# Chunk attention and a phase MLP on one core: fp32 weight loads on SyncE's queue, merged q/k copies, and a new written order

## The chip, the cores and the metric

The kernel runs on one core of one Trainium2 chip. The metric is the device time of one execution in microseconds (us). A core has five engines that run at the same time, each through its own list of instructions in order: TensorE (PE in the profile; PEld is its weight load), VectorE (DVE), ScalarE (ACT), GpSimd (POOL) and SyncE (SP). Transfers are issued from the POOL and SP queues here. An engine waits for another's result only where an instruction says so.

## The reference

Inputs are q, k and v of shape (8 batches, 8 heads, 576 rows, 64), and four weights. Attention runs inside chunks of 64 rows, with no link between chunks. Its result, seen as (8, 576, 512), goes through a phase MLP that mixes all 576 rows of a batch:

```python
scores = scale * np.matmul(q_c, k_c.transpose(0, 1, 2, 4, 3))   # per chunk of 64 rows
attn = np.exp(scores - max); attn = attn / (np.sum(attn) + 1e-09)
x = np.matmul(attn, v_c)                                        # -> (8, 576, 512)
theta = x @ w_theta
zr, zi = x * np.cos(theta), x * np.sin(theta)
y = einsum('ts,bsd->btd', w_tok_r, zr) + einsum('ts,bsd->btd', w_tok_i, zi)
u = x + y
out = u + np.maximum(u @ w_ch, 0.0)
```

w_theta and w_ch are 512 x 512, w_tok_r and w_tok_i 576 x 576. All inputs and the output are fp32 in HBM; the kernel computes in fp16 with fp32 sums.

## The kernel before, in words

**Tiling.** Batches are taken in four pairs, 0 to 3. A pair has 2 x 576 rows, which is nine tiles of 128 rows by 512 columns. Tiles 0 to 3 belong to the first batch, 5 to 8 to the second, and tile 4 holds the last 64 rows of both. Loads and attention work on five groups of a pair: A (tiles 0, 1), B (2, 3), M (4), C (5, 6) and D (7, 8).

**The order is written out by hand.** The string `ORDER` (L18) is a list of steps, and the loop at its end (L568) emits them one by one, with `work` (L525) as the table from a step's name to its function. A step such as `T.0M.1` is kind T, pair 0, group M, PSUM slot 1; `Y.05.1` is pair 0, tile 5. Each engine and each queue runs its own instructions in the order in which this list emits them, so a step that waits holds everything behind it on its engine. Nothing is reordered later.

**The steps of a group.** `q`, `k`, `v` (L170, L179) load from HBM on POOL's queue, and the transfer casts fp32 to fp16; each step is two DMAs. `T` (L250) transposes q and k of a group on PE into one PSUM tile. `tq` and `tk` (L268) copy the q half and the k half of that tile to SBUF, q on DVE, k on ACT (both on DVE for group M). `S` (L281) makes the scores, `e` (L297) their exp on ACT, `V0` and `V1` (L310) multiply with v for four heads each, and `v0` and `v1` (L329) divide by the sum on DVE, which gives x. `X` (L346) transposes x on PE, and `x` (L361) copies it out on ACT; or `Xd` (L370) does both as one DMA transpose on SP's queue. `H` (L381) is x times w_theta, `g` (L397) its cosine and sine on ACT, `z` (L412) the two products on DVE, and `zm` (L428) moves two half tiles for group M by DMA.

**The steps of a tile.** `Y` (L438) sums nine products of the transposed token weights with zr and zi; at the start of the kernel it is cut into `Ya`, `Yb`, `Yc`. `y` (L462) adds x on DVE and gives u. `U` (L469) transposes u on PE and `u` (L484) copies it out, on DVE for odd tiles and ACT for even ones; or `Ud` (L479) does it by DMA on SP's queue. `W` (L493) is u times w_ch, `w` (L503) is the relu and the last sum on DVE, and `st` (L511) stores with two DMAs on SP's queue.

**The weights.** `lw.00` (L187) loads all of w_tok_r in fp32 on SP's queue, and `cw` (L197) casts it on ACT; `lw.01` loads w_tok_i on POOL's queue with a cast. `TW` (L206) transposes the token weights on PE, three 128-row blocks of the result at a time, into one PSUM tile; `twd` and `twa` (L232) copy it out on DVE and ACT. `lt` and `lc` (L201) load w_theta and w_ch on POOL's queue with a cast. `D` (L154) is two blank matmuls of 512 columns, whose result nobody reads. `init` (L139) makes the identity for the transposes, on POOL.

**Buffers.** PSUM has three tiles of two banks (slots 0 to 2 of T, S, V, X, H, TW) and two of one bank (slots 0 and 1 of Y, U, W, D). SBUF tiles come from rings: seven for loaded q and k, six for u, four for the transposed u. A new use of a ring's buffer waits until its last reader is done.

The softmax here doesn't subtract the row's maximum and nothing guards it: scores larger than these inputs give would overflow.

## Time and profile before

| | |
|---|---|
| median of 4 runs | 212.46 us (211.46 to 213.87) |
| the profiled execution | 211.46 us, its span 209.7 us |
| PE busy | 190.5 us, 91% of the span |
| DVE busy | 123.5 us, 59% |
| ACT busy | 111.3 us, 53% |
| POOL busy | 104.3 us, 50% |
| moved by DMA | 31.36 MB, of which 15.88 MB on POOL's queue (with a cast) |
| q, k and v loads | 120 DMAs on POOL's queue, some 0.87 us each to issue |

The span runs from the first to the last instruction of the core. "Busy" is the time in which an engine had an instruction under way. The chain that ended last is followed back from the last instruction, at each step to what released it.

### The profile page before, as it was taken

How to read it: one execution, taken by the hardware profiler on the slowest of the kernel's cores; microseconds unless marked ns; L12 is line 12 of the kernel's file. 1: busy time of each engine (PE TensorE's matmuls, PEld its weight loads, DVE VectorE, ACT ScalarE, POOL GpSimd, SP SyncE). 2: the span in 40 equal slices, each digit the busy share in tenths (PEclk: the TensorE clock that was granted, in tenths of full speed). 3: DMA queues.
4: the chain of work that ended last, by engine and by line, in shares of the span. 5: the costliest groups of instructions: out<-in, count | busy, mean ns of one | idle time of the engine just before them, and what ended most of it. 6: DMA issues, size and time to landing. Idle time of an engine off the chain costs nothing.

```text
span 209.7 us, 6370 instructions
## 1 busy us (share of the span) xinstructions
PE 190.5 (91%) x2774; PEld 96.2 (46%) x2774; DVE 123.5 (59%) x240; ACT 111.3 (53%) x119; POOL 104.3 (50%) x130
## 2 busy tenths in 40 slices
PE   7797698897989999999999999998999979999981
PEld 2335354454545555455544545444544424444430
DVE  0015646464958756677885356949876465846351
ACT  2516587845796588777558668785250531500010
POOL 8998889997997789798998300000000000000000
PEclk9958799999999999999999999999999999999998
DMA  6999999999999999999999992425228687636875
GB/s 190 189 149 172 186 155 163 161 155 156 151 158 202 213 144 172 165 178 157 178 191 194 173 184 52 105 50 103 54 64 174 125 173 147 152 64 129 175 155 129
DMA packets 136858, 31.36 MB, mean 150 GB/s; under 512 B 129536, under 2 KB 131648, under 8 KB 136832
## 3 DMA queue, kind: packets, MB, share of 16 engines
q0 software_dynamic: 114176, 15.88, 120.1%
q1 hardware_dynamic: 22656, 15.10, 31.5%
q8 instruction: 21, 0.34, 0.7%
q14 instruction: 5, 0.04, 0.1%
HBM read 33.06 MB, written 9.44 MB: 203 GB/s over the span
## 4 chain that ended last, share of the span: by engine, by line
PE 65%; DVE 9%; ACT 9%; DMA 7%; POOL 6%; issue 1%; SPq 0%; POOLq 0%; ACTq 0%
PE ps_y L457 27%; PE ps_theta L388 14%; PE ps_uw L497 13%; POOL qk L174 5%; DMA v<-in_v_dram 4%; PE ps_x L323 3%; DMA xT<-x 3%; ACT kT L277 3%; PE ps_qkT L259 3%; PE ps_sT L290 2%; DVE qT L277 2%; DVE x L336 2%; PE ps_xT L354 2%; ACT xT L366 1%; PE ps_uT L474 1%
## 5 line engine op out<-in xcount | busy, mean ns | idle before, releaser
L457 PEld LDWEIGHTS <-wT 128*128 128x128 f16 (+1 forms) x360 | 30.7, 100 | 34.5 <-issue 0.8
L457 PE MATMUL ps_y<-zr,wT 128*128 128x512 f16 (+1 forms) x180 | 44.3, 381 | 0.0
L457 PE MATMUL ps_y<-zi,wT 128*128 128x512 f16 (+1 forms) x180 | 42.0, 379 | 0.0
L465 DVE TENSOR_TENSOR u<-ps_y,x 128x512 f16<-128x512 f32 x36 | 24.7, 689 | 27.9 <-PE ps_y L457 27.8
L497 PE MATMUL ps_uw<-wch,uT 128*128 128x512 f16 x144 | 36.3, 380 | 1.2 <-ACT uT L491 0.7
L388 PE MATMUL ps_theta<-wtheta,xT 128*128 128x512 f16 x144 | 35.1, 386 | 1.7 <-DMA xT<-x 1.3
L174 POOL DMA_DIRECT2D qk<-in_q_dram x40 | 34.2, 872 | 4.9 <-DMA qk<-in_q_dram 1.3
L174 POOL DMA_DIRECT2D qk<-in_k_dram x40 | 33.9, 868 | 4.8 <-DMA v<-in_v_dram 1.4
L182 POOL DMA_DIRECT2D v<-in_v_dram x40 | 34.1, 872 | 3.0 <-DMA qk<-in_k_dram 1.3
L506 DVE SCALAR_TENSOR_TENSOR o<-ps_uw,u 128x512 f32<-128x512 f32 x36 | 24.8, 688 | 16.1 <-PE ps_uw L497 15.8
L404 ACT ACTIVATE cos<-ps_theta,pihalf 128x1024 f16<-128x1024 f32 (+1 forms) x20 | 20.6, 1032 | 21.7 <-PE ps_theta L388 15.2
L303 ACT ACTIVATE eT<-ps_sT 128x1024 f16<-128x1024 f32 (+1 forms) x20 | 18.4, 938 | 16.5 <-PE ps_sT L290 16.4
L336 DVE TENSOR_TENSOR x<-ps_x,recip 128x512 f16<-128x512 f32 (+1 forms) x40 | 25.5, 638 | 1.4
L388 PEld LDWEIGHTS <-xT 128*128 128x128 f16 x144 | 13.4, 99 | 17.6 <-DMA xT<-x 2.3
L497 PEld LDWEIGHTS <-uT 128*128 128x128 f16 x144 | 13.0, 98 | 16.7 <-DMA uT<-u 1.4
L277 ACT COPY kT<-ps_qkT 128x1024 f16<-128x1024 f16 x16 | 16.1, 1018 | 7.8 <-DVE qT L277 4.4
L366 ACT COPY xT<-ps_xT 128x1024 f16<-128x1024 f16 (+1 forms) x15 | 13.9, 931 | 10.8 <-PE ps_xT L354 10.7
L408 ACT ACTIVATE sin<-ps_theta 128x1024 f16<-128x1024 f32 (+1 forms) x20 | 18.7, 937 | 0.0
L491 ACT COPY uT<-ps_uT 128x512 f16<-128x512 f16 x9 | 5.3, 592 | 24.3 <-PE ps_uT L474 24.2
L277 DVE COPY qT<-ps_qkT 128x1024 f16<-128x1024 f16 x16 | 11.0, 688 | 9.2 <-ACT kT L277 6.6
L259 PE MATMUL ps_qkT<-id,qk 64*128 64x64 f16 x576 | 12.8, 196 | 1.2 <-ACT sin L408 0.8
L335 DVE RECIPROCAL recip<-ps_x 128x8 f32<-128x8 f32 (+1 forms) x40 | 7.8, 196 | 9.9 <-PE ps_x L323 9.6
(43 smaller groups left out, 152.8 us busy)
## 6 DMA issues: line engine op xcount, KB each, us to landing
out_dram<-o SPq DMA_DIRECT2D x72, 128.0 KB, 2.5
qk<-in_q_dram POOLq DMA_DIRECT2D x32, 128.0 KB, 7.0
qk<-in_k_dram POOLq DMA_DIRECT2D x32, 128.0 KB, 7.0
v<-in_v_dram POOLq DMA_DIRECT2D x32, 128.0 KB, 6.7
wraw<-in_moe_w_tok_r_dram SPq DMA_DIRECT2D x1, 1152.0 KB
wnat<-in_moe_w_tok_i_dram POOLq DMA_DIRECT2D x1, 576.0 KB, 7.9
qk<-in_q_dram POOLq DMA_DIRECT2D x8, 64.0 KB, 6.4
qk<-in_k_dram POOLq DMA_DIRECT2D x8, 64.0 KB, 6.2
```

The source lines that it names most:

```text
L174: nc.gpsimd.dma_start(nats[p, g][rows, which, r], (q, k)[which][b, :, t0 : t0 + n, :].rearrange("h s d -> s h d"),)
L182: nc.gpsimd.dma_start(v16[rows, slot + r, :, 0:D], v[b, :, t0 : t0 + n, :].rearrange("h s d -> s h d"),)
L259: nc.tensor.transpose(psv[:, r, w, e, j, :], t[half[r], w, j, 2 * e : 2 * e + 2, :].rearrange("s h d -> s (h d)"), id16[half[r], half[r]],)
L277: copy(out=t.rearrange(flat), in_=ps.rearrange(flat))
L336: nc.vector.tensor_tensor(out=st[p]["x"][:, j0 : j0 + n, f * NE * D : (f + 1) * NE * D].rearrange("p c (h d) -> p c h d", h=NE), in0=psv[: ...
L388: nc.tensor.matmul(ps[:, j * DM : j * DM + DM], xT[:, j * NDB + db, :], wtheta16[:, db, :], start=(db == 0), stop=(db == NDB - 1),)
L404: nc.scalar.activation(out=cos[:, 0:n].rearrange("p a e -> p (a e)"), in_=pin, func=AF.Sin, bias=pihalf, scale=1.0,)
L408: nc.scalar.activation(out=sin[:, 0:n].rearrange("p a e -> p (a e)"), in_=pin, func=AF.Sin)
L457: nc.tensor.matmul(ps[rows], wT[:, kt, cols], z[:, jz, :], start=(kt == 0), stop=(kt == 2 * KT),)
L465: nc.vector.tensor_tensor(out=u, in0=st[p].pop(("ps_y", j))[:, 0:DM], in1=st[p]["x"][:, j], op=ALU.add)
L497: nc.tensor.matmul(ps, uT[:, db * P : db * P + P], wch16[:, db, :], start=(db == 0), stop=(db == NDB - 1),)
L506: nc.vector.scalar_tensor_tensor(out=o, in0=st[p].pop(("ps_uw", j)), scalar=0.0, in1=u, op0=ALU.max, op1=ALU.add)
```

## The change

The change has six parts.

1. **Token weights.** `load_tok` now has four steps. `lw.00` and `lw.01` load rows 0 to 255 of w_tok_r and w_tok_i in fp32 on SP's queue; `lw.02` and `lw.03` load the other rows (256 to 511, and 512 to 575) on POOL's queue with a cast. `cw.00` and `cw.01` cast the fp32 halves on DVE. The fp32 tile borrows the buffer that pair 1's zr uses later. `TW` has four steps, two for each part of the rows, and all its copies (`twd`) are on DVE; `twa` is gone.
2. **Phase weight.** `lt` loads w_theta in fp32 on SP's queue, into the buffer that pair 1's x uses later, and `ct` casts it on ACT.
3. **q and k copies.** The two copies of a transposed group become one over the whole PSUM tile: `tq` on DVE (15 groups), `tqa` on ACT (5 groups). `Td`, a DMA transpose of q and k, is defined but the order doesn't use it.
4. **Other copies.** The copy of transposed x is on DVE in nine groups (`xv`) and on ACT in five (`x`); group 2B is transposed by DMA (`Xd.2B`). The copy of transposed u is on ACT (`ua`) or DVE (`uv`) by the order's choice, eight each. The tiles whose u goes by DMA are others, still 20.
5. **Blank matmuls.** A `D` step is one blank matmul instead of two, and there are 60 steps instead of 14.
6. **Order and rings.** The order is written anew on all engines and queues, with `init` after the first eight loads on POOL's queue and group 0D's q ahead of group 0A's v; the ring of loaded q and k has 8 buffers (7 before), that of u 7 (6), that of transposed u 5 (4).

```diff
--- before.py
+++ after.py
@@ -16,50 +16,52 @@
 
 
 ORDER = """
-ones.00 D.00.0 lw.00 cw.00 D.00.1 init.00 D.00.0 D.00.1 q.0M q.0B q.0A D.00.0 k.0M
-D.00.1 D.00.0 D.00.1 k.0B TW.00.0 twa.00 k.0A D.00.0 T.0M.1 tk.0M D.00.1 D.00.0 tq.0M
-S.0M.2 e.0M lt.00 T.0B.1 T.0A.2 tk.0A tq.0B D.00.1 tq.0A tk.0B S.0A.2 v.0M V1.0M.1 v.0A
-e.0A D.00.0 V0.0M.2 twd.00 S.0B.0 new.00 v1.0M V1.0A.1 v0.0M V0.0A.2 v0.0A v.0B q.1M
-v1.0A lw.01 X.0M.2 e.0B V1.0B.0 X.0A.1 v1.0B x.0M H.0M.2 V0.0B.0 x.0A v0.0B q.0C k.1M
...
-W.38.1 w.38 st.38 D.00.0
+ones.00 D.00.0 D.00.1 lw.01 cw.01 lw.00 D.00.0 q.0M D.00.1 D.00.0 D.00.1 D.00.0 D.00.1
+D.00.0 D.00.1 D.00.0 q.0B q.0A cw.00 k.0M D.00.1 D.00.0 D.00.1 D.00.0 D.00.1 D.00.0
+D.00.1 lt.00 init.00 D.00.0 D.00.1 D.00.0 TW.00.0 twd.00 TW.01.1 D.00.1 D.00.0 D.00.1
+D.00.0 D.00.1 k.0B v.0M D.00.0 k.0A T.0M.2 tq.0M S.0M.0 D.00.1 twd.01 D.00.0 D.00.1 v.0B
+D.00.0 q.0D D.00.1 D.00.0 D.00.1 T.0B.2 new.00 D.00.0 D.00.1 e.0M ct.00 V1.0M.1 tq.0B
+v.0A q.0C q.1M D.00.0 D.00.1 v1.0M S.0B.0 V0.0M.2 v0.0M k.0D T.0A.1 lw.02 X.0M.2 tq.0A
+e.0B V1.0B.0 lw.03 x.0M v1.0B S.0A.2 k.1M H.0M.1 e.0A D.00.0 D.00.1 g.0M V0.0B.0 D.00.0
+D.00.1 D.00.0 D.00.1 v0.0B X.0B.2 x.0B k.0C V1.0A.0 v1.0A D.00.0 D.00.1 V0.0A.1 v0.0A
+X.0A.0 v.0D xv.0A H.0B.2 H.0A.1 q.1D v.0C lc.00 g.0B T.0D.0 z.0M q.1A tq.0D D.00.0 k.1D
...
+Ud.35 W.35.0 Ud.37 st.38 W.36.1 w.35 st.35 w.36 st.36 W.37.0 U.30.1 uv.30 w.37 W.30.1
+D.00.0 D.00.0 D.00.0 D.00.0 st.37 w.30 st.30 D.00.1 D.00.0 D.00.1 D.00.0 D.00.1 D.00.0
@@ -112,7 +114,7 @@
     thin = ctx.enter_context(
         tc.tile_pool(name="thin", bufs=1, space=bass.MemoryType.PSUM)
     )
-    nat = ctx.enter_context(tc.tile_pool(name="nat", bufs=7))
+    nat = ctx.enter_context(tc.tile_pool(name="nat", bufs=8))
     tmp = ctx.enter_context(tc.tile_pool(name="tmp", bufs=3))
     pairp = ctx.enter_context(tc.tile_pool(name="pairp", bufs=1))
     outp = ctx.enter_context(tc.tile_pool(name="outp", bufs=4))
@@ -131,8 +133,6 @@
     wch16 = glob.tile([P, NDB, DM], FP16, name="wch16")
     wT = glob.tile([P, 2 * KT + 1, S], FP16, name="wT")
     wnat = glob.tile([P, KT + 1, 2, S], FP16, name="wnat")
-    wraw = pairp.tile([P, KT, S], FP32, name="wraw")
-    wend = glob.tile([CH, S], FP32, name="wend")
     blank = const.tile([P, DM], FP16, name="blank")
     v16 = glob.tile([P, 2 * NT, H, VP], FP16, name="v16")
@@ -153,8 +153,7 @@
     def idle(p, i, slot):
         ps = psum1("ps_idle", slot)
-        for r in range(2):
-            nc.tensor.matmul(ps, blank[:, 0:P], blank, start=True, stop=True)
+        nc.tensor.matmul(ps, blank[:, 0:P], blank, start=True, stop=True)
@@ -184,66 +183,77 @@
                 v[b, :, t0 : t0 + n, :].rearrange("h s d -> s h d"),
             )
-    def load_tok(ri):
+    def load_tok(i):
+        part, ri = divmod(i, 2)
         ap = (moe_w_tok_r, moe_w_tok_i)[ri]
-        aps = ap[0 : KT * P, :].rearrange("(a p) s -> p a s", p=P), ap[KT * P : S, :]
-        if ri == 0:
-            nc.sync.dma_start(wraw, aps[0])
-            nc.sync.dma_start(wend, aps[1])
-        else:
-            nc.gpsimd.dma_start(wnat[:, 0:KT, 1], aps[0])
-            nc.gpsimd.dma_start(wnat[0:CH, KT, 1], aps[1])
-    def cast_tok():
-        nc.scalar.copy(out=wnat[:, 0:KT, 0], in_=wraw)
-        nc.scalar.copy(out=wnat[0:CH, KT, 0], in_=wend)
+        if part == 0:
+            if "tok32" not in st:
+                st["tok32"] = pairp.tile([P, 2, 2, S], FP32, name="tok32", tag="zr1")
+            nc.sync.dma_start(
+                st["tok32"][:, :, ri], ap[0:GT, :].rearrange("(a p) s -> p a s", p=P)
+            )
+            return
+        nc.gpsimd.dma_start(
+            wnat[:, 2 * part : 2 * part + 2, ri],
+            ap[part * GT : part * GT + GT, :].rearrange("(a p) s -> p a s", p=P),
+        )
+        nc.gpsimd.dma_start(wnat[0:CH, KT, ri], ap[KT * P : S, :])
+    def cast_tok(i):
+        nc.vector.tensor_copy(out=wnat[:, 0:2, i], in_=st["tok32"][:, :, i])
     def load_w(ap, f16):
         nc.gpsimd.dma_start(f16, ap.rearrange("(a p) e -> p a e", p=P))
-    def tok_w(k3, slot):
+    def load_theta():
+        st["theta32"] = pairp.tile([P, NDB, DM], FP32, name="theta32", tag="x1")
+        nc.sync.dma_start(st["theta32"], moe_w_theta.rearrange("(a p) e -> p a e", p=P))
+    def cast_theta():
+        nc.scalar.copy(out=wtheta16, in_=st["theta32"])
+    def tok_w(i, slot):
+        part = i // 2
+        kts = range(KT) if i % 2 == 0 else range(KT, 2 * KT + 1)
+        n = len(kts)
         ps = psum2("ps_wT", slot, FP16)
-        for k in range(3):
-            kt = 3 * k3 + k
-            for tb in range(KT + 1):
-                rows = slice(0, P if tb < KT else CH)
-                if tb < KT:
-                    at = k * KT * P + (tb // 2) * GT + (tb % 2) * CH
-                    to = ps[:, at : at + GT].rearrange("p (c r x) -> p c r x", c=2, r=2)
-                    to = to[:, :, 0]
-                else:
-                    at = 3 * KT * P + k * CH
-                    to = ps[:, at : at + CH]
-                for h in range(2):
-                    if kt < 2 * KT:
-                        ri, jl = kt // KT, kt % KT
-                        s0 = (jl // 2) * GT + (jl % 2) * CH + h * P
+        main = ps[:, 0 : n * GT].rearrange("p (k x) -> p k x", k=n)
+        middle = ps[:, 5 * GT : 5 * GT + n * CH].rearrange("p (k x) -> p k x", k=n)
+        for tbs in ((0, 1),) if part == 0 else ((2, 3), (KT,)):
+            for k, kt in enumerate(kts):
+                for tb in tbs:
+                    rows = slice(0, P if tb < KT else CH)
+                    if tb < KT:
+                        to = main[:, k].rearrange("p (c r x) -> p c r x", c=2, r=2)
+                        to = to[:, :, tb % 2]
                     else:
-                        ri, s0 = h, KT * P
-                    nc.tensor.transpose(
-                        to[half[h]],
-                        wnat[rows, tb, ri, s0 : s0 + CH],
-                        id16[rows, rows],
-                    )
-        st["wT", k3] = ps
-    def tok_w_copy(k3, r):
-        ps = st["wT", k3]
-        ks = slice(3 * k3, 3 * k3 + 3)
-        most = ps[:, 0 : 3 * KT * P].rearrange("p (k x) -> p k x", k=3)
-        if r == 0:
-            c = slice(0, GT)
-        else:
-            c = slice(GT, KT * P)
-        eng = nc.scalar.copy if r else nc.vector.tensor_copy
-        eng(out=wT[:, ks, c], in_=most[:, :, c])
-        if r == 0:
-            eng(
-                out=wT[:, ks, KT * P : S],
-                in_=ps[:, 3 * KT * P : 3 * S].rearrange("p (k c) -> p k c", k=3),
-            )
+                        to = middle[:, k]
+                    for h in range(2):
+                        if kt < 2 * KT:
+                            ri, jl = kt // KT, kt % KT
+                            s0 = (jl // 2) * GT + (jl % 2) * CH + h * P
+                        else:
+                            ri, s0 = h, KT * P
+                        nc.tensor.transpose(
+                            to[half[h]],
+                            wnat[rows, tb, ri, s0 : s0 + CH],
+                            id16[rows, rows],
+                        )
+        st["wT", i] = main, middle
+    def tok_w_copy(i):
+        main, middle = st["wT", i]
+        part = i // 2
+        ks = slice(0, KT) if i % 2 == 0 else slice(KT, 2 * KT + 1)
+        nc.vector.tensor_copy(out=wT[:, ks, part * GT : part * GT + GT], in_=main)
+        if part:
+            nc.vector.tensor_copy(out=wT[:, ks, KT * P : S], in_=middle)
@@ -265,22 +275,37 @@
                         )
         st[p]["ps_qkT", g] = psv
-    def qk_copy(p, g, which):
+    def qk_tile(n):
+        return tmp.tile(
+            [P, 4 * NE * n * CH], FP16, name="qkT", tag=f"qkT{n}",
+            bufs=4 if n == 2 else 2,
+        )
+    def qk_copy(p, g, copy):
         n = 1 if g == "M" else 2
-        ps = st[p]["ps_qkT", g][:, :, which]
-        name = "qk"[which] + "T"
-        t = tmp.tile([P, 2, NE, n, CH], FP16, name=name, tag=f"{name}{n}", bufs=n + 1)
-        st[p][name, g] = t
-        copy = nc.scalar.copy if which and n == 2 else nc.vector.tensor_copy
-        if n == 2:
-            flat = "p r e j c -> p r (e j c)"
-            copy(out=t.rearrange(flat), in_=ps.rearrange(flat))
+        ps, t = st[p]["ps_qkT", g], qk_tile(n)
+        tv = t.rearrange("p (r w e j c) -> p r w e j c", r=2, w=2, e=NE, j=n)
+        if n == 1:
+            flat = "p r w e c -> p (r w e) c"
+            copy(out=tv[:, :, :, :, 0].rearrange(flat), in_=ps[:, :, :, :, 0].rearrange(flat))
         else:
-            copy(out=t[:, :, :, 0], in_=ps[:, :, :, 0])
+            copy(out=t, in_=ps.rearrange("p r w e j c -> p (r w e j c)"))
+        st[p]["qkT", g] = lambda hs, w, e, j, r: tv[hs, r, w, e, j, :]
+    def qk_dma(p, g):
+        t = qk_tile(2)
+        nc.sync.dma_start_transpose(
+            t.rearrange("p (a c) -> p a c", c=P),
+            nats.pop((p, g)).rearrange("p w j h d -> p (w j h d)"),
+        )
+        tv = t.rearrange("p (w j e r c) -> p w j e r c", w=2, j=2, e=NE, r=2)
+        st[p]["qkT", g] = lambda hs, w, e, j, r: tv[hs, w, j, e, r, :]
     def scores(p, g, slot):
         n = 1 if g == "M" else 2
-        qT, kT = st[p].pop(("qT", g)), st[p].pop(("kT", g))
+        t = st[p].pop(("qkT", g))
         ps = psum2("ps_sT", slot)
         psv = ps.rearrange("p (h j e c) -> p h j e c", h=2, j=2, e=NE)
         for j in range(n):
@@ -289,8 +314,8 @@
                     for r in range(2):
                         nc.tensor.matmul(
                             psv[half[r], h, j, e, :],
-                            kT[half[h], r, e, j, :],
-                            qT[half[h], r, e, j, :],
+                            t(half[h], 1, e, j, r),
+                            t(half[h], 0, e, j, r),
                         )
         st[p]["ps_sT", g] = ps
@@ -358,12 +383,12 @@
                     )
         st[p]["ps_xT", g] = psv
-    def x_copy(p, g):
+    def x_copy(p, g, copy):
         n = 1 if g == "M" else 2
         psv = st[p].pop(("ps_xT", g))
         xT = tmp.tile([P, 2 * NDB, P], FP16, name="xT")
         st[p]["xT", g] = xT
-        nc.scalar.copy(
+        copy(
             out=xT[:, 0 : n * NDB].rearrange("p a (r c) -> p r a c", r=2), in_=psv
         )
@@ -460,7 +485,7 @@
                 )
     def add_x(p, j):
-        u = tmp.tile([P, DM], FP16, name="u16", bufs=6)
+        u = tmp.tile([P, DM], FP16, name="u16", bufs=7)
         st[p]["u", j] = u
         nc.vector.tensor_tensor(
             out=u, in0=st[p].pop(("ps_y", j))[:, 0:DM], in1=st[p]["x"][:, j], op=ALU.add
@@ -477,18 +502,15 @@
         st[p]["ps_uT", j] = psv
     def u_dma(p, j):
-        uT = tmp.tile([P, DM], FP16, name="uT", bufs=4)
+        uT = tmp.tile([P, DM], FP16, name="uT", bufs=5)
         st[p]["uT", j] = uT
         nc.sync.dma_start_transpose(uT.rearrange("p (a c) -> p a c", a=NDB), st[p]["u", j])
-    def u_copy(p, j):
-        uT = tmp.tile([P, DM], FP16, name="uT", bufs=4)
+    def u_copy(p, j, copy):
+        uT = tmp.tile([P, DM], FP16, name="uT", bufs=5)
         st[p]["uT", j] = uT
         psv = st[p].pop(("ps_uT", j))
-        if j % 2:
-            nc.vector.tensor_copy(out=uT, in_=psv)
-        else:
-            nc.scalar.copy(out=uT, in_=psv)
+        copy(out=uT, in_=psv)
     def w(p, j, slot):
         uT = st[p].pop(("uT", j))
@@ -526,19 +548,20 @@
         "q": lambda p, g: load_qk(p, g, 0),
         "k": lambda p, g: load_qk(p, g, 1),
         "v": load_v,
-        "lt": lambda p, g: load_w(moe_w_theta, wtheta16),
+        "lt": lambda p, g: load_theta(),
+        "ct": lambda p, g: cast_theta(),
+        "cw": lambda p, i: cast_tok(i),
         "lc": lambda p, g: load_w(moe_w_ch, wch16),
         "lw": lambda p, i: load_tok(i),
-        "cw": lambda p, i: cast_tok(),
         "init": lambda p, g: setup(),
         "ones": lambda p, g: fill(),
         "new": lambda p, g: pair(p),
         "TW": lambda p, i, slot: tok_w(i, slot),
-        "twd": lambda p, i: tok_w_copy(i, 0),
-        "twa": lambda p, i: tok_w_copy(i, 1),
+        "twd": lambda p, i: tok_w_copy(i),
         "T": qk_t,
-        "tq": lambda p, g: qk_copy(p, g, 0),
-        "tk": lambda p, g: qk_copy(p, g, 1),
+        "Td": qk_dma,
+        "tq": lambda p, g: qk_copy(p, g, nc.vector.tensor_copy),
+        "tqa": lambda p, g: qk_copy(p, g, nc.scalar.copy),
         "S": scores,
         "e": exps,
         "V0": lambda p, g, slot: attn(p, g, 0, slot),
@@ -547,7 +570,8 @@
         "v1": lambda p, g: norm(p, g, 1),
         "X": x_t,
         "Xd": x_dma,
-        "x": x_copy,
+        "x": lambda p, g: x_copy(p, g, nc.scalar.copy),
+        "xv": lambda p, g: x_copy(p, g, nc.vector.tensor_copy),
         "H": theta,
         "g": trig,
         "z": phase,
@@ -560,7 +584,8 @@
         "y": add_x,
         "U": u_t,
         "Ud": u_dma,
-        "u": u_copy,
+        "ua": lambda p, j: u_copy(p, j, nc.scalar.copy),
+        "uv": lambda p, j: u_copy(p, j, nc.vector.tensor_copy),
         "W": w,
         "w": relu_add,
         "st": store,
```

## The prediction

> **What bounds the kernel now.** I read the engine totals first, then the slices, the windows, the chain that ended last, and the waits. The page of the profiled execution:
>
> ```profile
> span 209.7 us, 6370 instructions
> PE 190.5 (91%) x2774; PEld 96.2 (46%) x2774; DVE 123.5 (59%) x240; ACT 111.3 (53%) x119; POOL 104.3 (50%) x130
> PE   7797698897989999999999999998999979999981
> PEclk9958799999999999999999999999999999999998
> DMA  6999999999999999999999992425228687636875
> ```
>
> PE is the only engine near its span. Its weak stretch is the first seven slices, where the granted clock falls too; DMA is full until slice 24, then light. The windows answer splits the span where the first Y matmul starts (35.45 us) and after the last W:
>
> ```profile
> 0.00:35.40 35.40, 27.99 (x432) 14.40 (x432) 11.76 (x30) 18.96 (x20) 31.42 (x45) 0.86 2.09 173
> 35.40:205.00 169.60, 162.20 (x2344) 81.81 (x2344) 111.14 (x211) 92.31 (x99) 72.85 (x86) 1.00 1.43 146
> 205.00:209.70 4.70, 0.27 (x2) 0.00 (x0) 0.57 (x1) 0.00 (x0) 0.00 (x0) 0.83 0.54 119
> ```
>
> The columns after the window's length are the busy us of PE, PEld, DVE, ACT and POOL, then clock, DMA share and GB/s. After 35.4 PE is idle for 169.60-162.20 = 7.4 us only. Before it, 35.4 us hold 28.0 busy, of which 10.5 (6.33+4.13, the same view cut down to line 157) are blank matmuls: half of the start is no work. So there are two pools to gain from, about 18 us of start-up and 7.4 us of gaps; the last 4.7 us are a relu_add and a store. The chain's shares by line, and two lines of the waits (who waited for whom: us, times, longest), name the gaps:
>
> ```profile
> PE ps_y L457 27%; PE ps_theta L388 14%; PE ps_uw L497 13%; POOL qk L174 5%; DMA v<-in_v_dram 4%; PE ps_x L323 3%; DMA xT<-x 3%; ACT kT L277 3%; PE ps_qkT L259 3%; PE ps_sT L290 2%; DVE qT L277 2%; DVE x L336 2%; PE ps_xT L354 2%; ACT xT L366 1%; PE ps_uT L474 1%
> ```
>
> ```profile
> DVE qT L277 <- ACT kT L277: 6.6, 7, 1.4
> ...
> ACT kT L277 <- DVE qT L277: 4.4, 2, 3.5
> ```
>
> The q and k halves of one transposed group are copied by two engines, but one after the other: 7 times VectorE waits for ScalarE's copy and twice the reverse. At the start the chain, in order of time (start, us, what), runs through loads:
>
> ```profile
> 1.44 6.39 POOL qk L174 x8
> ...
> 14.56 7.62 DMA v<-in_v_dram
> ```
>
> The v rows of group 0A land at 22.2 us and everything downstream hangs on them; the line "POOL qk" is the queue that feeds them.
>
> **What the Trainium skill says.** "DMA: Bandwidth & Descriptors", section "Issuing engines are not separate DMA queues": SP's and POOL's transfers share the same 16 engines. So the theta weight on SP's queue still takes engine time from POOL's loads; the trace agrees in that q0's packets alone took 120.1% of 16 engines' span. The same page, "Queues, rings and completion order": engines alternate between rings at packet granularity. "TensorE: Matmul & The Clock Gate", Part 1: the array is throttled until busy for some 3.4 us. The trace agrees in kind, not in size: blank matmuls start 0.43 us apart until 6.7 us and 0.2 after, 5.5 us in, and half rate returns at 13.2 and 25.1 us. "VectorE: DVE Perf Modes", the perf-mode tier table: an fp32 copy within SBUF runs at up to 2x, a 16-bit copy from PSUM at up to 2x; the trace's 1024-column PSUM copy at 688 ns against 414 for 512 columns agrees with the second and shows nothing of the first.
>
> **The change, part by part.** *q/k copies.* A big group (16 of them) loses one ACT copy (1.018) and one DVE copy (0.688), done in turn: 1.71 us. It gets one copy of 2048 columns: on DVE 0.688+2x0.274 = 1.24 us (slope from 414 and 688), on ACT (1C, 2A, 3A, 3B) 1.018+2x0.42 = 1.86 (slope from 598 and 1018). In the chain, in order of time, this serial pair stands seven times after 35.4 us, with 10.0 us in all; 6 whole groups at 1.71-1.24 = 0.47 give **-2.8 us**. Bounds: 0 where PE had other queued work, -4.5 if a PSUM slot freed sooner lets PE go on as well.
>
> *VectorE's load.* Copies: 12x1.24+3x0.688-14.3 = +2.6. Nine xT copies move over: 8x0.688+0.414 = +5.9. One uT copy more: +0.4. wT copies 0.69+0.83+0.97+1.14 against 2.4: +1.2. Two casts of 1152 fp32 columns appear in no row; the page's 2x rate gives an estimate of 0.76 us each, one element per cycle 1.35: +1.5 to 2.7, I take 1.5. Sum 123.5+11.6 = **135 us**. ScalarE: -16.1+7.4+1.0 (k), -9.7 (x), -0.6 (u), -2.4 (wT), -2.8+1.9 (casts; 2048 columns from the row of 2304 at 2.11), and the order alternates 12 times between Exp and Sin where it was 14, -2x1.28. Sum 111.3-23.9 = **87 us**. In the dense part VectorE goes from 111 of 169.6 us to some 121, 71%: hidden on average, but it is one in-order queue, and a late copy there holds the PE step behind it. I charge **+0.5 us**, bounds 0 and +10.
>
> *Start-up loads.* SP issues both halves of rows 0-255 and theta at 0.7 us, 2.2 MB against 1.3. POOL loses theta's issue (0.80), gains a second pair of token loads (0.76+0.54), and starts 0.7 us sooner because the identity now follows k.0M. A 128 KB load moves in about 1 us (15.88 MB in some 120 us). Up to v.0A the stream held 17 such units, theta as 4 of them by bytes (2 if its longer packets go faster); it now holds 17 without theta, because q.0D is put ahead. SP's extra 0.9 MB costs nothing to 4.0 us (0.9 MB at the 227 GB/s that the windows give for 1.2 to 9 us). So v.0A lands between 22.2-0.7 = 21.5 and 22.2+2+4.0-0.7 = 27.5; I take 23.5. From there PE's order has V, two normalisations (2x0.9), X, H.0B (1.73, over the xT copy of H.0A), H.0A 1.73, T.0D 1.06, TW.02 1.2, S.0D 0.35, TW.03 1.5, T.1M 0.55 and four blanks: first Y at 35.0. TW.03 also needs the second token load, 10.6 units behind v.0A by bytes (34.1 us), which could hold Y until 36.4; I take 35.5. That is no sooner than 35.45, but T.0D and S.0D (1.4 us) are behind it: **-1.4 us**, bounds -3.9 and +2.2 (first Y at 33.0 or 39.0). The first transposes of token weights are not what is late: both fp32 halves (1.18 MB) land like the 1.15 MB of before, at 6.8 us, and the two casts end by 8.3 to 9.5, where TW.00 began at 8.94.
>
> *Blanks.* 28 blank matmuls become 60. The 21 ahead of TW.00 run 13x0.43+8x0.2155 = 7.3 us and end at 8.5, under the load's cover. Some 27 more lie in waits up to 35 us; where a wait is shorter they delay work, 0.22 us each. Their gain is the clock: 12 theta matmuls and the small ones between 10 and 30 us ran partly at half rate. I leave it at nothing; it is a reserve of at most 2 us. Ten at the end need some 2.2 us beside the last store's issue and landing (about 4): 0, or up to 1 us if the cover is short.
>
> *Late transposes.* X.2B goes to SP's queue: -16 transposes, **-0.4 us**. The number of u transposes on the DMA stays 20, only others: SP's queue has five 1.2 us store pairs at its end as before. Buffers (8 for q/k, 7 u, 5 uT): 0; POOL's 0.9 us wait on a score matmul may go. Borrowing pair 1's x and zr for the fp32 weights costs nothing: they are written long after.
>
> Sum: -2.8+0.5-1.4-0.4 = **-4.1 us**. Against this execution, span 209.7 and 1.8 around it (211.46), that is 205.6 and 207.4. Its time lies 1.0 below the median of the runs, 212.46; there the forecast is **208.4 us**, own range 205.5 to 210.3. About 1% is what a measurement here can tell from no change.
>
> **Rivals.** *More is taken*: v.0A lands early (-3.9) and the gaps shrink by 5 rather than 2.3, with -0.4: -9.3, 203.2 us. For it: 18 us of start-up hold no work, and clock loss is uncounted. Against: the loads set the pace there, and the bytes stay the same. *Nothing is gained*: the loads come at their late bound (+2.2 where -1.4 was taken) and eat the rest, -4.1+3.6 = -0.5, 212.0 us. For it: in the first 30 us the DMA engines are full and SP adds to them. Against: theta leaves POOL's stream. *Slower, by VectorE's queue*: of the 11.6 us added, more than 4.6 (the gains) on PE's path means no gain; with 8 on it the time is 212.46-4.6+8 = 215.9 us. It decides where steps that PE waits for (v0, v1, tq, y) stand behind several 0.69 and 1.24 us copies. Against: VectorE stays 29% idle there, and ScalarE's waits go. That the change doesn't do what it says: the fp32 loads could land late and hold the casts at the head of VectorE's queue, and tq.0M behind them; that is within the +2.2.
>
> **Chances.** Forecast 0.50, more 0.14, nothing 0.20, VectorE 0.16. Faster than 1% is the first two, 0.64; within 0.20; slower 0.16. The range, 203.5 to 214.5, takes in all but the VectorE case and the far edge of "more", about 0.2.
>
> **What would show it.** The row of DVE copies from ps_qkT at 1.2 us and no wait between kT and qT; first Y near 35 us with T.0D done; PE idle from there under 6 us; DVE near 135 and ACT near 87. I am wrong if the v.0A landing moves past 26 us, or if PE's waits on DVE from ps_qkT, recip and x exceed 4 us.

## The result, and the profile after

The changed kernel takes **212.81 us** (median of 35 runs) where the kernel before, beside it on the same chips, takes 212.74 (56 runs): a ratio of 0.9999, interval [0.9981, 1.0016]. Nothing that can be measured was gained; 208.4 was forecast. The profiled execution took 212.05 us with a span of 210.3, so against the 211.46 and 209.7 of before it is 0.6 us longer; most of that is the choice of execution, since the one before lies 1.3 us under its median and this one 0.8. All ratios below are to the kernel before on the same chip, with a 95% interval. A ratio leaves out the executions that took over 1.5% more than the fastest of the same kernel, at most half of them (six of twelve in a_theta_late), while the medians are of all.

The page of the changed kernel: engine totals, the slices of PE and its clock, and the row of the merged copy:

```profile
PE 192.7 (92%) x2790; PEld 96.2 (46%) x2790; DVE 134.3 (64%) x243; ACT 89.2 (42%) x91; POOL 105.0 (50%) x131
PE   7928879999999989998999999977979999999995
PEclk9996999999999999999999999999999999999999
...
L294 DVE COPY qkT<-ps_qkT 128x2048 f16<-128x2048 f16 x12 | 14.6, 1217 | 5.0 <-PE ps_qkT L269 4.9
```

The work moved as the prediction had it: VectorE at 134.3 (135 forecast), ScalarE at 89.2 (87), a merged copy at 1.217 us (1.24). PE's clock is nearly whole from the first slice but for slice 4 (15.8 to 21.0 us), yet PE is thin in slice 3 (10.5 to 15.8 us) and, late, in slices 27, 28 (136.7 to 147.2) and 30. The windows, cut at the first Y matmul and 5.2 us before the end (columns as in the prediction):

```profile
0.00:37.78 37.78, 29.49 (x519) 14.99 (x520) 16.98 (x32) 15.17 (x16) 33.22 (x46) 0.95 2.00 178
37.78:205.10 167.32, 160.57 (x2263) 80.48 (x2262) 116.64 (x211) 74.06 (x76) 71.83 (x86) 1.00 1.40 147
205.10:210.30 5.20, 2.69 (x11) 0.76 (x8) 0.69 (x1) 0.00 (x0) 0.00 (x0) 1.00 0.64 141
```

The same cuts of before hold 35.45, 169.05 and 5.2 us, with PE busy 161.65 in the middle one. So Y starts 2.33 us later (with T.0D and S.0D, 0.57 and 0.38 us on the chain, already done), and PE is still idle for 6.75 us after that, where it was 7.4. What changed is **who it waits for**. PE's waits from the first Y on, first before (waiter, awaited, us in total, times, longest):

```profile
PE ps_theta L388 <- DMA xT<-x: 1.3, 2, 1.0
PE ps_sT L290 <- DVE recip L335: 1.3, 1, 1.3
PE ps_x L323 <- ACT eT L303: 0.9, 1, 0.9
PE ps_sT L290 <- ACT kT L277: 0.8, 1, 0.8
PE ps_qkT L259 <- ACT sin L408: 0.8, 1, 0.8
PE ps_uw L497 <- ACT uT L491: 0.7, 1, 0.7
PE ps_uw L497 <- DMA uT<-u: 0.5, 1, 0.5
...
```

and then after:

```profile
PE ps_uw L519 <- DMA uT<-u: 2.6, 1, 2.6
PE ps_theta L413 <- DMA xT<-x: 1.8, 2, 1.5
PE ps_qkT L269 <- DMA qk<-in_k_dram: 0.9, 2, 0.6
PE ps_x L348 <- DMA v<-in_v_dram: 0.7, 1, 0.7
PE ps_uw L519 <- DVE uT L513: 0.5, 1, 0.5
```

With three lines of 0.3 us each that are left out, before has 5.4 us of waits for ScalarE and VectorE and 1.8 for DMAs; after has 0.5 and 6.0. The new order takes 4.9 us of engine waits away, and 4.2 us of waits for transfers come in their place. The largest is one event. SP's queue around it (start, us, instruction), and PE's line:

```profile
137.34 1.44 SPq L400 DMA_TRANSPOSE xT<-x  x1
138.90 6.13 SPq L507 DMA_TRANSPOSE uT<-u  x4
...
143.17 1.04 PE L519 MATMUL ps_uw<-wch,uT 128*128 128x512 f16 x4 [2.64 <-DMA uT<-u]
```

`Xd.2B` goes out at 137.34, behind four stores on the same queue, and `Ud.27` right behind it at 138.90; the chain of the changed kernel puts the latter's landing 4.23 us later, at 143.13, and W.27 waits.

The start hangs on another load than I thought. PE's transposes of group 0M's k rows, first before, then after, and two pieces of the chain after, in order of time (start, us, what):

```profile
12.90 0.39 PE L259 MATMUL ps_qkT<-id,qk 64*128 64x64 f16 x7 [0.30 <-DMA qk<-in_k_dram]
...
14.83 0.20 PE L269 MATMUL ps_qkT<-id,qk 64*128 64x64 f16 x1 [3.40 <-DMA qk<-in_k_dram]
```

```profile
7.30 8.15 DMA qk<-in_k_dram
...
17.00 2.79 PE ps_idle L156 x7
```

The k rows of group 0M (`k.0M`) land at 15.45 us; before, PE had them at 12.90. After a wait of 3.4 us for their first half the clock falls to half, and the seven blanks behind S.0M take 0.40 us each; 16 theta matmuls of the same 512 columns take 3.56 us on the chain later, 0.22 each.

What held `k.0M` up can be read from the two queues. q0 is POOL's, q1 is SP's; packets, MB and share of the 16 engines' time from 2 to 8 us, first before, then after:

```profile
q0 software_dynamic: 2299, 0.29, 75.6%
q1 hardware_dynamic: 597, 1.30, 65.1%
...
q1 hardware_dynamic: 845, 1.79, 90.2%
q0 software_dynamic: 428, 0.05, 13.9%
```

While SP's fp32 loads run, POOL's queue hardly moves: 0.05 of 1.85 MB. SP's extra 0.9 MB, at the 380 GB/s that the trace gives from 3 to 6 us, are 2.4 us by my estimate, and `k.0M` comes 2.6 us later.

### The profile page after: what moved, and what is told of

It is laid out like the page before. It is cut to its first block, busy times and chain, and to the rows that moved or that the text cites. A ratio compares the mean times of both kernels' runs of the same rounds, so it can differ in the third digit from the quotient of the medians.

```text
span 210.3 us, 6378 instructions
## 1 busy us (share of the span) xinstructions
PE 192.7 (92%) x2790; PEld 96.2 (46%) x2790; DVE 134.3 (64%) x243; ACT 89.2 (42%) x91; POOL 105.0 (50%) x131
## 4 chain that ended last, share of the span: by engine, by line
PE 67%; DMA 16%; POOL 8%; DVE 3%; issue 3%; SPq 2%; ACT 0%; POOLq 0%
PE ps_y L482 28%; PE ps_theta L413 11%; PE ps_uw L519 11%; DMA qk<-in_k_dram 8%; POOL qk L173 5%; PE ps_qkT L269 4%; PE ps_idle L156 4%; DMA qk<-in_q_dram 3%; DMA xT<-x 3%; POOL v L181 3%; PE ps_x L348 3%; PE ps_sT L315 3%; DMA uT<-u 2%; PE ps_uT L499 1%; PE ps_xT L379 1%
## 5 line engine op out<-in xcount | busy, mean ns | idle before, releaser
L482 PE MATMUL ps_y<-zr,wT 128*128 128x512 f16 (+1 forms) x180 | 45.0, 380 | 0.0
L413 PE MATMUL ps_theta<-wtheta,xT 128*128 128x512 f16 x144 | 33.9, 379 | 1.8 <-DMA xT<-x 1.8
L156 PE MATMUL ps_idle<-blank 128*128 128x512 f16 x60 | 19.0, 447 | 1.4 <-DVE pihalf L144 1.2
L294 DVE COPY qkT<-ps_qkT 128x2048 f16<-128x2048 f16 x12 | 14.6, 1217 | 5.0 <-PE ps_qkT L269 4.9
L269 PE MATMUL ps_qkT<-id,qk 64*128 64x64 f16 x576 | 12.4, 191 | 4.9 <-DMA qk<-in_k_dram 4.8
L269 PEld LDWEIGHTS <-qk 64*128 64x128 f16 x576 | 9.9, 95 | 9.2 <-DMA qk<-in_k_dram 5.3
L348 PE MATMUL ps_x<-v,eT 64*64 64x65 f16 x576 | 11.2, 196 | 0.8 <-DMA v<-in_v_dram 0.7
```

Source lines behind the costliest of these rows:

```text
L156: nc.tensor.matmul(ps, blank[:, 0:P], blank, start=True, stop=True)
L269: nc.tensor.transpose(psv[:, r, w, e, j, :], t[half[r], w, j, 2 * e : 2 * e + 2, :].rearrange("s h d -> s (h d)"), id16[half[r], half[r]],)
L413: nc.tensor.matmul(ps[:, j * DM : j * DM + DM], xT[:, j * NDB + db, :], wtheta16[:, db, :], start=(db == 0), stop=(db == NDB - 1),)
L482: nc.tensor.matmul(ps[rows], wT[:, kt, cols], z[:, jz, :], start=(kt == 0), stop=(kt == 2 * KT),)
```

## The experiments

Three accounts could explain the missing 4 us. The **start** account: theta's megabyte on SP's queue, issued at once, delays `k.0M` and all behind it. The **copies** account: the 2.8 us charged to merging the q and k copies never was on PE's path. The **new waits** account: the gains were there, but DMA transposes and loads take them back. A fourth suspect is the blank matmuls.

### One part alone, put into the kernel before

**b_merge: merged copies in the old order.** In the kernel before, each first step of a `tq`/`tk` pair becomes the merged copy, the second is dropped; the same five groups are copied by ScalarE.

```diff
-T.0B.1 T.0A.2 tk.0A tq.0B D.00.1 tq.0A tk.0B S.0A.2
+T.0B.1 T.0A.2 tq.0A tq.0B D.00.1 S.0A.2
```

> The kernel before with one part of the change: the q and k copies of a group merged into one (15 on VectorE, the same five on ScalarE), at the place of the first of the two; its order and all else stay. The prediction's step: -2.8 us, ratio 0.985 to 0.990, and PE idle after the first Y down from 7.4 to about 5 us. Rival V (VectorE's longer queue eats it): the waits on ScalarE's copy go, waits of PE on VectorE's copies and on x come up, ratio 0.997 to 1.005.

Measured: 214.91 us, ratio 1.0113 [1.0042, 1.0184]: **slower**. Its windows from the first Y on, and the largest of PE's waits there:

```profile
38.02:206.60 168.58, 161.16 (x2341) 81.09 (x2340) 112.84 (x202) 87.59 (x90) 70.90 (x84) 1.00 1.38 144
...
PE ps_theta L390 <- ACT sin L410: 2.7, 1, 2.7
```

PE is idle for 168.58-161.16 = 7.42 us there, against 7.40. The waits for kT, qT and recip are gone, and one of 2.7 us for the sine has come. The loss of this execution lies in the start, where the first Y moves to 38.02. Two groups, tk.0A beside tq.0B, were copied by two engines at once there and are now copied one after the other on VectorE. That this is the reason is not shown: PE also waits 2.0 us for v loads there (0.2 before), and its granted clock in the start is 0.78 (0.86).

**b_merge_late: the same, only behind group 1M.** The four groups at the start keep two copies on two engines.

```diff
-T.0C.0 e.1M Yb.03 tq.0C Yc.03 tk.0C S.0C.2
+T.0C.0 e.1M Yb.03 tq.0C Yc.03 S.0C.2
```

> The kernel before with merged q/k copies in the 16 groups after 1M alone; 0M, 0A, 0B and 1M, whose copies lie ahead of the first Y, stay split. The prediction's step (-2.8 us in the dense part): ratio 0.985 to 0.990, PE idle after the first Y near 5 us. What the merge in all groups showed (idle after the first Y unchanged at 7.4 us, the loss ahead of it): ratio 0.997 to 1.003, first Y at 35 to 36 us.

Measured: 215.18 us, 1.0076 [1.0051, 1.0101]. With the copies of the start as they were, the kernel is slower by 0.8% all the same, so the merge at the start is not the whole reason. Where the loss stands is not shown: the only profile is of one of the longest executions (216.32 us), with its first Y at 36.98 and a clock of 0.77 in the start, though the copies there are untouched.

**b_theta_sp: theta in fp32 on SP's queue at once.** Nothing else of the change.

```diff
-ones.00 D.00.0 lw.00 cw.00 ... S.0M.2 e.0M lt.00
+ones.00 D.00.0 lw.00 lt.00 cw.00 ... S.0M.2 e.0M ct.00
```

> The kernel before with one part of the change: the phase weight in fp32 on SP's queue at once, behind the token weights, cast by ScalarE after the first exp; POOL's stream loses it. Theory S: k.0M lands 2 us later (near 15 us) and v.0A about where it was, since POOL's stream is 1 MB shorter; first Y within 1 us of 35.45, ratio 0.997 to 1.006. Theory G (the move is a gain by itself, hidden in the change by other losses): v.0A lands 2 us sooner, first Y near 33.5, ratio 0.988 to 0.994.

Measured: 215.06 us, 1.0089 [1.0064, 1.0115]. PE's timeline at the wait (start, us, instruction, idle before it):

```profile
15.23 0.23 PE L266 MATMUL ps_qkT<-id,qk 64*128 64x64 f16 x1 [3.66 <-DMA qk<-in_k_dram]
15.69 0.39 PE L266 MATMUL ps_qkT<-id,qk 64*128 64x64 f16 x7 [0.22 <-DMA qk<-in_k_dram]
```

The second half of `k.0M` is there at 15.69, 2.8 us later than before (2.6 in the changed kernel), which is what theta's 1.05 MB take at the 380 GB/s above, by my estimate; the first Y is at 37.35, and PE's idle time after it is unchanged (7.45). This one move costs 0.9%.

### One part undone, in the changed kernel

**a_theta_pool: theta back on POOL's queue with a cast.**

```diff
-D.00.1 lt.00 init.00 ... k.0A T.0M.2 ... e.0M ct.00 V1.0M.1
+D.00.1 init.00 ... k.0A lt.00 T.0M.2 ... e.0M V1.0M.1
```

> The changed kernel, but with the phase weight loaded on POOL's queue with a cast behind k.0A, as the kernel before does, and without ScalarE's cast of it. Theory S (theta's 1 MB on SP's queue takes the engines from POOL's first loads): k.0M lands near 13 us in place of 15.5 and the first Y starts 1 to 2.5 us sooner, ratio 0.988 to 0.996. Theory B (the bytes are the same wherever they are issued): k.0M sooner, but v.0B, v.0A and the token weights as late as before or later by theta's turn in the stream, first Y within 0.7 us, ratio 0.997 to 1.005.

Measured: 214.66 us, 1.0086 [1.0057, 1.0115]. `k.0M` comes soon (its transposes start at 11.43), but theta now stands ahead of v.0B and v.0A on POOL's queue, and the first Y is at 39.08, later than the changed kernel's 37.78. In this order theta costs something on either queue, and less on SP's.

**a_theta_late: theta on SP's queue, held back.** VectorE writes one column of theta's buffer behind `twd.00`, and the load waits for that.

```diff
-D.00.1 lt.00 init.00 D.00.0 D.00.1 D.00.0 TW.00.0 twd.00 TW.01.1
+D.00.1 init.00 D.00.0 D.00.1 D.00.0 TW.00.0 twd.00 ht.00 lt.00 TW.01.1
```

> The changed kernel, with theta's load on SP's queue held back until VectorE has copied the first transposed token weights (about 10 us), by a one-column write of its tile on VectorE ahead of the load. The same bytes on the same queue, only later. Theory S (theta in the first 10 us delays k.0M, and the start hangs on k.0M): k.0M lands near 13 us in place of 15.5, theta by 18 us, ahead of its use at 24.7; first Y 1 to 2.5 us sooner than 37.8, ratio to the kernel before 0.988 to 0.995. Theory B (the sum of bytes ahead of v.0A and the token weights sets the start): k.0M sooner, first Y within 0.7 us of 37.8, ratio 0.997 to 1.003.

Measured: 214.37 us, 0.9999 [0.9955, 1.0042]. The twelve executions run from 211.04 to 216.89 us, so this shows that nothing was gained, and no more. `k.0M` comes at 11.93, 3.5 us sooner than with theta at once, and the first Y at 38.34, no sooner. The delay only moves to the loads behind, first to k of group B:

```profile
18.90 0.55 PE L273 MATMUL ps_qkT<-id,qk 64*128 64x64 f16 x14 [3.59 <-DMA qk<-in_k_dram]
```

**a_theta_quarter: a quarter of theta's bytes.**

```diff
-nc.sync.dma_start(st["theta32"], moe_w_theta.rearrange("(a p) e -> p a e", p=P))
+nc.sync.dma_start(st["theta32"][:, 0], moe_w_theta[0:P, :])
```

> The changed kernel with three quarters of theta's load left out: SP loads 128 of the 512 rows, and the cast writes these four times, so the output is not the reference's. It prices 0.75 MB in the first 10 us. Theory B and theory S both: k.0M lands about 2 us sooner. Theory B: the whole stream behind moves by the same, v.0A and the token weights 2 us sooner, first Y near 35.5 to 36, ratio 0.988 to 0.993. Theory D (after k.0M the start is a chain of dependent steps and blanks on PE that loads don't touch): first Y 2 to 2.5 us sooner all the same, since k.0M heads that chain; it is told from B by where PE's waits on v and on token weights go: none before, none after. If first Y moves by less than 1 us, loads are not what sets the start.

Measured: 209.15 us, 0.9868 [0.9806, 0.9931]. Its windows:

```profile
0.00:34.27 34.27, 28.48 (x520) 14.87 (x521) 17.26 (x33) 15.60 (x16) 32.13 (x45) 1.00 1.93 168
34.27:201.50 167.23, 161.12 (x2264) 80.62 (x2263) 116.98 (x211) 73.63 (x76) 73.24 (x87) 1.00 1.41 148
```

The first Y comes 3.5 us sooner, `k.0M` at 12.7, and the part behind it is as long as in the changed kernel (167.23 against 167.32). So fewer bytes make the start sooner where a later load does not, and 0.75 MB are worth 1.3%. At the 380 GB/s above they are 2 us by my estimate. The rest of the 3.5 us is not separated; the clock, whole in this start (1.00 against 0.95), is one candidate.

**a_noblank: no blank matmuls between TW.01 and the first Y** (28 of the 60).

```diff
-TW.01.1 D.00.1 D.00.0 D.00.1 D.00.0 D.00.1 k.0B v.0M D.00.0 k.0A
+TW.01.1 k.0B v.0M k.0A
```

> The changed kernel without the 28 blank matmuls that stand between the first two steps of token-weight transposes and the first Y (the 21 at its head and the ten at its end stay). Theory P (the blanks stand on the path: after the changed profile, 5.3 us of its chain from 17 to 38 us are blanks, seven of them run at 0.4 us each before T.0B): first Y near 33 to 35 us in place of 37.8, ratio to the kernel before 0.980 to 0.990. Theory C (the blanks buy the clock): the transposes and the 12 theta matmuls run at half rate again, first Y where it was or later, ratio 0.998 to 1.01. Theory L (loads set the pace): first Y unmoved, the blanks' time turns into waits on q, k and v transfers, ratio 0.998 to 1.002.

Measured: 212.32 us, 0.9968 [0.9943, 0.9993]. The theta matmuls of the start, row by line, engine and operation, as busy us and mean ns:

```profile
L411 PE MATMUL ps_theta<-wtheta,xT 128*128 128x512 f16 x20 | 8.1, 585 | 0.0
```

In the changed kernel the same 20 take 4.7 us, 380 ns each. The blanks do keep the clock up, and the first Y comes at 39.81 without them. But PE's wait for uT shrinks from 2.6 to 1.5 us when the start is later, and the total comes out within 0.3%.

**a_split: two copies on two engines, in the changed kernel's order.** VectorE copies q, ScalarE k, in place of each merged copy.

```diff
-T.0B.2 ... tq.0B v.0A
+T.0B.2 ... tq.0B tk.0B v.0A
```

> The changed kernel with the q/k copies split again as before: q on VectorE and k on ScalarE for big groups, both on VectorE for group M; the order's place of each stays. Theory of the prediction (a merged copy saves 0.47 us where it stands on the path): 1 to 2.8 us slower than the changed kernel, ratio 1.005 to 1.013. Theory Z (two engines side by side are as good as one copy, as the merge put into the kernel before showed): ratio 0.995 to 1.003, and VectorE some 6 us less busy.

Measured: 231.27 us, 1.0813 [1.0755, 1.0871]. Its waits:

```profile
ACT kT L293 <- DVE qT L293: 23.8, 10, 5.6
...
PE ps_sT L308 <- ACT kT L293: 11.6, 7, 4.0
```

ScalarE stands idle for 23.8 us until VectorE's q half is done: all 16 k halves begin only after the q half of their group has ended, as the pair ran in turn before. At other times ScalarE's half is late itself, behind cosines and sines (a q half copied at 57.28 us gets its k half at 61.38), and the scores wait. Two copies side by side were thus not tested; two copies in turn were. So the new order needs the merged copy, while the old order is slower with it: what the merge is worth lies in the order, and cannot be read from the pair of copies alone.

### The DMA transposes

**a_u27: tile 27 transposed on PE and copied by VectorE.**

```diff
-S.3B.1 Ud.27 e.3B Ud.15
+S.3B.1 U.27.1 uv.27 e.3B Ud.15
```

> The changed kernel, with u of tile 27 transposed on PE and copied by VectorE, in place of the DMA transpose whose landing PE waits 2.6 us for at 143 us. Theory T (that wait is a loss of its own): PE idle after the first Y falls from 6.75 to about 4.5 us, PE gets 0.3 us of transposes, ratio 0.989 to 0.993. Theory N (the next wait takes its place: H.2B, behind the W of tile 27 in PE's order, waits for x of group 2B, whose DMA transpose stands just ahead on the same queue): ratio 0.997 to 1.002.

Measured: **208.16 us, 0.9797 [0.9765, 0.9830]**, faster than both kernels. The windows of this kernel, and PE's longest waits in the middle one:

```profile
0.00:38.17 38.17, 30.98 (x519) 15.60 (x520) 17.00 (x32) 15.16 (x16) 34.67 (x48) 0.91 2.09 180
38.17:201.60 163.43, 160.23 (x2267) 80.33 (x2266) 116.89 (x212) 73.90 (x76) 70.74 (x84) 1.00 1.41 149
...
PE ps_theta L414 <- DMA xT<-x: 1.8, 2, 1.2
PE ps_qkT L270 <- issue: 0.6, 1, 0.6
```

The start is no better, and PE's idle time after the first Y falls from 6.75 to 3.2 us. The wait for uT is gone.

**a_u27_again: the same kernel, timed again on another chip.**

> The kernel with u of tile 27 transposed on PE once more, with more runs. The first time it had 4 runs and 0.980, where the wait that it takes away is 2.6 us, 1.2%. If 0.980 is its size: 0.977 to 0.983, and the trace should show about 2 us more than that wait. If chance gave part of it: 0.984 to 0.990.

Measured: 208.98 us, 0.9785 [0.9754, 0.9817]. The gain of 2.1% stands. The named wait of 2.6 us explains 1.2%. Some 1.6 us more in the profiles is load waits between 60 and 100 us (PE busy 18.84 and 19.37 of 20 us in those two windows of the changed kernel, 19.78 and 20.00 in a_u27), which lie ahead of the edit. They are not tile 27's: the profiles of a_x2b and a_u27_x2b below have 19.78 and 20.00 there too, and these kernels gain 0.4%. What makes the rest of the 2.1% stays open.

**a_x2b: group 2B transposed on PE and copied by ScalarE**, tile 27 left on the DMA.

```diff
-st.11 Xd.2B v1.3A z.2A tqa.3B S.3B.1 Ud.27
+st.11 v1.3A z.2A tqa.3B S.3B.1 X.2B.2 x.2B Ud.27
```

> The changed kernel with x of group 2B transposed on PE and copied by ScalarE again, in place of the DMA transpose that the change puts on SP's queue just ahead of the one of tile 27. Theory Q (it is the queue: tile 27's transpose landed 4.2 us after its issue because group 2B's, twice as large, ran ahead of it): PE's wait for tile 27 shrinks from 2.6 to about 1 us, PE gets 0.4 us of transposes, ratio to the kernel before 0.991 to 0.996. Theory N (a step of tile 27 that waits for its own latency): the wait stays, ratio 1.000 to 1.004.

Measured: 212.63 us, 0.9958 [0.9932, 0.9983]. PE's waits behind the first Y:

```profile
PE ps_theta L414 <- DMA xT<-x: 2.1, 2, 1.2
PE ps_uw L520 <- DMA uT<-u: 1.9, 3, 1.3
PE ps_xT L380 <- DVE x L362: 0.8, 1, 0.8
```

Tile 27's transpose now goes out at 136.30 as the first of its row, and W.27 starts at 141.27 without a wait for it. The three waits for uT in the list (1.9 us) are of other tiles, from 172 us on, and X.2B waits 0.8 us for x.

**a_u27_x2b: both on PE**, the edits of a_u27 and a_x2b together.

> The changed kernel with both transposes, u of tile 27 and x of group 2B, on PE. If late DMA transposes are the loss: ratio 0.977 to 0.983, as good as tile 27 alone or 0.2% better. If PE's 0.7 us of transposes outweigh what is left to gain: 0.1 to 0.4% slower than tile 27 alone.

Measured: 211.87 us, 0.9959 [0.9938, 0.9979]. With tile 27 on PE, moving 2B there too gives back 1.7 of the 2.1%; with 2B on PE, moving tile 27 brings nothing (0.9958 and 0.9959). The two do not add. The DMA form of 2B is the right one; the transpose behind it is not. The size of 2B alone does not make the one behind it late: here a 128x512 goes first (2.6 us to landing), and the 128x512 right behind it, at 137.53, still takes 4.2 us. What does make it late, the place in the row or the stores ahead on the queue, is not separated; at 163.29 in the changed kernel a 128x512 right behind a 128x1024 took 2.5.

### Combined with the start

These four start from a_u27. The loads variant puts v.0A ahead of q.0D, and q.0C and q.1M behind the second token loads; "late" holds theta back as above.

```diff
-v.0B D.00.0 q.0D ... v.0A q.0C q.1M ... lw.03 x.0M
+v.0B D.00.0 ... v.0A q.0D ... lw.03 q.0C q.1M x.0M
```

> The changed kernel with u of tile 27 transposed on PE (0.980 by itself) and without the 28 blank matmuls between the first token-weight transposes and the first Y (0.997 by themselves). If the two add: ratio 0.975 to 0.979. If the 0.980 held a chance part beside the 2.6 us wait that it names (2.6 us are 1.2%): 0.983 to 0.988.

a_u27 without the 28 blanks (the edit of a_noblank): 211.46 us, 0.9918 [0.9895, 0.9942]; first Y 39.33. Here the blanks are worth 1.2%. That they were worth nothing in the changed kernel fits a wait for tile 27 that swallowed the gain; this is argued, not shown.

> The changed kernel with tile 27's transpose on PE, and with another order on POOL's queue: v.0A ahead of q.0D, and q.0C and q.1M behind the last token weights. v.0A and the token weights come 2 and 3 us sooner in the stream. Theory D (after k.0M the start is a chain of dependent steps and blanks, and loads don't touch it): first Y where it was, 37.5 to 38.2, ratio 0.979 to 0.984, as without the new order. Theory B (the loads behind k.0M set the pace too): first Y near 36, ratio 0.970 to 0.976.

New load order: 210.24 us, 0.9865 [0.9794, 0.9936]; first Y 38.19 against 38.17. v.0A sooner brings nothing.

> As the last one, and theta's load held back until about 10 us, so that k.0M lands near 12 us. With both, k.0M is early and v.0A and the token weights have fewer bytes ahead. Theory D and B together (k.0M heads the chain, and the bytes behind it caught the held-back theta up): first Y 34.5 to 36.5, ratio 0.966 to 0.975. If theta's bytes only push k.0B and v.0M back: first Y 37.5 or later, 0.979 to 0.984.

With theta held back too: 211.93 us, 0.9937 [0.9908, 0.9965]; `k.0M` at 12.4, first Y at 40.55. As in a_theta_late, a sooner `k.0M` alone buys no sooner Y.

> As the last one, without the 28 blank matmuls. If k.0M lands early, PE's idle stretches are short and the clock holds without blanks: first Y 1 to 3 us sooner than with them, ratio 0.960 to 0.970. If the blanks hold the clock up: theta's matmuls of groups A and B run at half rate (6.1 us for 16, as without blanks before, against 3.6), first Y later by 1 to 2 us, and the end within 0.3% of the last one.

Without blanks as well: 213.73 us, 1.0027 [0.9995, 1.0060]; first Y 40.18. None of the three orders beats a_u27.

## Why the prediction was wrong

The sum, step by step against the profiled executions (forecast 207.4 from 211.46, measured 212.05):

| step | predicted | measured |
|---|---|---|
| start-up loads | -1.4 (first Y 35.5) | +1.4 (first Y 37.78, 0.95 of other work done) |
| copies, VectorE's load, X.2B: from the first Y on | -2.8+0.5-0.4 = -2.7 | -0.8 (167.32-169.05+0.95) |
| the last 5.2 us | 0 | 0 |
| sum | -4.1 | +0.6 |

**The start-up step failed.** It priced theta's bytes against v.0A and said that SP's extra 0.9 MB "costs nothing to 4.0 us" there, but `k.0M` was not in the sum. In the changed kernel the chain hangs on it: 12.9 to 15.5 us, and b_theta_sp shows 2.8 us with theta as its only edit. v.0A was not what PE waited for: it landed at 25.4 and 26.4 us, later than the 23.5 taken and its second half past the 26 named as a sign, but PE used it at 27.76 with no wait. T.0D and S.0D, counted as 1.4 us of work done early, take 0.95. The loss of 1.4 us is inside the stated bound (+2.2), and that was the rival "nothing is gained". Its total, 212.0 us, fits in part by luck: it had the loads at +2.2 and the gains in the dense part whole, where the start lost 1.4 and most of the gains did not come. "DMA: Bandwidth & Descriptors", section "Queues, rings and completion order", which the prediction cited, would have warned: it has an engine take turns between rings by the packet, from which I infer that long packets get the larger share. From 2 to 8 us SP's queue had 1.79 of 1.85 MB, in packets of some 2,100 bytes against POOL's 120. That POOL's queue stood back is shown; that the packets' length is why is argued. The prediction took its 120.1% for a sign that the two queues share the engines; that figure is of one queue and does not show it, and b_theta_sp does.

**The copies step failed.** It took the serial pair of copies in the chain, seven times, as time that PE would get back. In the old order, from which it was worked out, PE gets back nothing: b_merge leaves it idle for 7.42 us against 7.40, with a wait for the sine where those for the copies were, and b_merge_late is no faster. A stretch of the chain is a limit only while nothing else is nearly as late. In the new order engine waits did go, 4.9 us of them, more than I asked for; what the merge has in that cannot be told from the order's part.

**A step at nothing failed.** "The number of u transposes on the DMA stays 20, only others" was charged 0. Which tile it is matters: tile 27's stands behind group 2B's on one queue, with PE needing it at once. That is 2.6 us of named wait; taking it away is worth 2.1% in a_u27 and a_u27_again, of which the wait explains 1.2%. "X.2B to SP's queue" was charged -0.4 and looked at for PE alone, not for what is queued behind it. Together with 1.6 us of waits for k and v in this execution, which the prediction looked for at the start only, this ate what the order had saved.

**What held.** The engine totals; the copy's 1.2 us; no waits between the two halves; the first token transposes not late (the fp32 halves land 4.0 and 5.0 us after issue); the tail. VectorE's queue, the rival that would have made it slower, did not act: PE's waits for VectorE's qkT, x and uT are 3.1 us in the whole span, under the stated 4. The blanks are a wash, as charged, though not for lack of effect. "TensorE: Matmul & The Clock Gate", Part 1, has the array fall back after some 3.4 us without work; the 3.4 us wait for `k.0M` with half-rate blanks behind it agrees. The kernel before does not: its granted clock is 0.50 from 10.2 to 16.9 us, and PE's longest wait between 6.7 and 10.2 us is 1.4 us. There a shorter wait stood before the fall. "PE idle from there under 6 us" was wrong: 6.75.

## What to carry to other kernels

Price an early bulk load against the first transfer that PE needs, not only against the one on which the old chain hung, and count the bytes of the whole start: holding the load back moved the delay, and only fewer bytes removed it. Do not add up pieces of the chain as savings; ask of each what is late next. A transpose by DMA took 2.4 to 4.2 us from issue to landing in the changed kernel: give it to tiles with several microseconds before their use, and keep the tile that is needed next on PE.

## What the runs showed of the hardware

- A DMA transpose of 128x512 issued right behind one of 128x1024 on SP's queue landed 4.2 us after its issue; the quickest of the four around it took 2.4. Right behind a 128x512 (a_u27_x2b) another took 4.2 as well, and one right behind a 128x1024 at 163.29 us of the changed kernel took 2.5.
- A 1 MB fp32 load on SP's queue pushed the landing of group 0M's k rows, loaded by POOL's queue, from 12.9 to 15.7 us (b_theta_sp). From 2 to 8 us of the changed kernel SP's queue moved 1.79 MB and POOL's 0.05; in the kernel before, 1.30 and 0.29.
- The two copies of one transposed group, by VectorE and ScalarE out of the same PSUM tile, never overlapped in a_split: each of the 16 k halves began after its q half had ended.
- Two casts of the same shape on VectorE (128x1152, fp32 to fp16) took 1.20 and 0.76 us; nothing here says why the two differ.
- Theta's matmuls of 512 columns took 380 ns with blanks around them and 585 ns on average without.
